# A fused linear attention and MoE kernel: numerators in one PSUM bank and the free columns of the visitor's key-value bank, a visit in five operations, a new order

## The chip, the cores and the metric

The kernel runs on one core of a Trainium2 chip. The metric is the device time in microseconds of one execution. Each statement of a time below is from a run on the chip or from one profiled execution of it.

## What is computed

Per head, keys and queries go through a feature map with an exponential of both signs; keys and values are summed over the sequence into a small matrix kv and a vector z; each query gives a numerator (its features times kv) and a denominator (its features times z). The quotients of 8 batches and 8 heads, 576 tokens of 64 columns each, are the 4608 x 512 input of a feed-forward stage.

```python
def phi(x):
    proj = np.einsum('bhsd,df->bhsf', x, w_phi)
    proj = proj - np.max(np.abs(proj), axis=-1, keepdims=True)
    return np.concatenate([np.exp(proj), np.exp(-proj)], axis=-1)
q_p, k_p = (phi(q), phi(k))
kv = np.einsum('bhsf,bhsd->bhfd', k_p, v)
z = np.sum(k_p, axis=2)
num = np.einsum('bhsf,bhfd->bhsd', q_p, kv)
den = np.einsum('bhsf,bhf->bhs', q_p, z)[..., None] + 1e-06
x = (num / den)          # then 4608 tokens x 512
h = x @ w_in             # 512 -> 1024
e = np.exp(h - h_max); solu = h * e / (e.sum() + 1e-09)
out = layer_norm(solu) * g_ln @ w_out
```

## The kernel before

The attention is cut into 16 units u of four heads, and each unit into two pairs of heads (sub 0 and 1), so there are 32 pairs n = 2u + sub. For a pair, TensorE projects keys and queries (`k_rows`, `q_rows`, `mid_rows`; tiles pjk, pjq, pjm), VectorE takes row maxima off and turns the queries, ScalarE takes exponentials (ek, fq), GpSimd adds up z (zt, zacc), and TensorE makes kv (tile kvT). VectorE turns kv into kvs, SP sends it through DRAM and back as kvf. From the tenth pair on ScalarE and VectorE also make qz, the features weighted with z, for the denominators. TensorE then makes numerators and denominators, ScalarE copies them out (E, dn), VectorE takes reciprocals, SP broadcasts them (rb), and GpSimd divides into xa or xb. The feed-forward works on 36 tiles of 128 tokens: ScalarE and GpSimd split the input in two parts (mxh, mxl), TensorE makes h with 24 matmuls of 512 columns, VectorE and ScalarE make nm, eu and ub, and after a way through DRAM (uTs, uhs, uls) TensorE makes o with 24 more.

PSUM has six banks of 512 fp32 columns under tag a, and one double bank under tag h for h. A kv takes 384 columns of a bank (3F, with F = 128): 256 for kv and 128 for z.

All operations are declared to a `Plan` (L217) in a fixed sequence, each with its engine, what it comes after, and the buffers it takes and uses. `SEQUENCE` (L54) is a list of positions in that declaration: `order` (L235) emits the operations in that order and hands out buffers first in, first out, each when its last user stands earlier in the list. Every engine runs its own operations in that order (`InOrder`, L258), waiting at each for what it needs; a bank that is handed on makes the next user wait until the last reader of the former is done.

The unit of the work around the change is the visit (`visit`, L588), operation V of a pair. For the pairs 0 to 5 it makes kv alone. From pair 6 on (JOIN) a visit is joined: one undivided run on TensorE that holds the numerators of the pair before (`q_num`, L759: two halves of 288 columns, in two banks of tag a), the kv matmuls of its own pair (eight, 256 columns), for sub 0 the four matmuls over the tokens that the two pairs share (vz), the z sums (L617), and the denominators of the pair before (`q_den`, L790, a bank of its own). A joined visit with sub 0 takes five banks at once: two for numerators, two for kv (both pairs of the unit), one for denominators. `q_oe` (L812) copies numerators out in two steps c (qv), `den_eps` the denominators (de), `kv_turn` reads the kv bank (kve).

The visit is declared at L950 to L975, the numerators and denominators and their copies at L1040 to L1056.

Of the kernel before, what the change touches and what calls it, by code (L numbers as in the profile page):

```python
# [54 lines left out]
    2, 119, 1, 120, 77, 79, 93, 121, 122, 82, 83, 309, 86, 310, 131, 137, 134, 103, 104, 123, 124, 84, 94, 95,  # L55
    97, 96, 98, 99, 132, 138, 100, 133, 78, 88, 105, 106, 80, 81, 135, 136, 101, 102, 311, 312, 139, 10, 11, 85,
    125, 91, 185, 4, 5, 92, 176, 109, 126, 127, 128, 129, 130, 111, 112, 89, 90, 313, 107, 108, 211, 212, 215,
    110, 314, 169, 171, 174, 175, 113, 114, 87, 6, 261, 150, 178, 151, 156, 157, 153, 154, 152, 12, 13, 155,
    158, 213, 214, 216, 7, 115, 116, 28, 29, 217, 140, 142, 177, 143, 186, 141, 195, 172, 187, 190, 173, 8, 144,
    117, 145, 193, 194, 9, 118, 196, 189, 192, 223, 188, 226, 180, 183, 181, 30, 191, 218, 43, 44, 3, 221, 229,  # L60
    159, 160, 197, 198, 277, 182, 161, 184, 163, 162, 199, 200, 45, 14, 219, 220, 222, 268, 278, 279, 282, 284,
    22, 23, 280, 283, 46, 281, 224, 227, 31, 170, 201, 24, 25, 225, 228, 269, 231, 164, 179, 230, 203, 204, 202,
    146, 33, 263, 321, 242, 15, 245, 244, 247, 262, 248, 205, 206, 371, 243, 246, 249, 34, 289, 290, 207, 208,
    264, 270, 424, 272, 35, 209, 16, 250, 265, 26, 273, 274, 232, 165, 147, 148, 17, 32, 36, 210, 27, 275, 291,
    276, 315, 166, 18, 380, 233, 236, 237, 149, 167, 168, 38, 285, 286, 238, 425, 525, 251, 271, 322, 253, 266,
    267, 252, 426, 316, 427, 428, 287, 288, 255, 256, 19, 319, 37, 39, 40, 41, 429, 451, 292, 293, 294, 257, 20,
    21, 295, 302, 296, 317, 318, 418, 239, 240, 258, 259, 320, 344, 452, 364, 419, 420, 234, 235, 241, 297, 254,
    260, 48, 303, 47, 42, 49, 50, 323, 381, 382, 383, 421, 1849, 384, 1850, 51, 52, 59, 65, 385, 386, 392, 387,
    393, 366, 324, 325, 326, 422, 423, 327, 304, 345, 367, 328, 330, 331, 333, 369, 430, 370, 390, 368, 388,
    1891, 526, 529, 332, 1851, 329, 389, 74, 527, 528, 530, 68, 391, 298, 1852, 299, 300, 301, 56, 487, 373,  # L70
    375, 478, 488, 1853, 1854, 66, 1892, 378, 374, 489, 471, 491, 490, 431, 334, 335, 1855, 336, 372, 53, 54,
    57, 346, 347, 348, 349, 398, 399, 1858, 400, 305, 338, 1893, 432, 353, 1870, 350, 60, 351, 492, 494, 306,
    354, 307, 308, 339, 1894, 376, 377, 379, 365, 589, 71, 493, 1895, 598, 433, 434, 642, 1859, 62, 355, 537,
    453, 58, 352, 636, 499, 500, 394, 395, 401, 472, 1896, 1897, 1900, 1871, 404, 435, 340, 356, 69, 357, 454,
    538, 405, 406, 1898, 1901, 1872, 1873, 396, 341, 342, 75, 397, 402, 403, 440, 76, 358, 359, 437, 1856, 61,
    72, 438, 55, 1912, 1913, 337, 343, 455, 441, 407, 408, 409, 442, 582, 1874, 473, 474, 1902, 599, 475, 1875,
    1876, 1857, 600, 601, 713, 456, 603, 604, 410, 495, 1903, 436, 637, 496, 505, 1914, 638, 639, 602, 605, 67,
    63, 64, 476, 73, 1904, 1905, 1860, 1861, 439, 70, 480, 411, 1906, 1862, 1863, 477, 479, 539, 640, 540, 641,
    648, 443, 643, 445, 460, 360, 412, 413, 446, 497, 1879, 461, 498, 482, 485, 1907, 1915, 531, 541, 1908,
    1909, 591, 483, 644, 457, 484, 506, 414, 415, 416, 361, 481, 507, 646, 458, 645, 1916, 459, 501, 502, 508,  # L80
    590, 486, 444, 1899, 447, 417, 751, 647, 1864, 1917, 1918, 1919, 1921, 673, 362, 363, 704, 462, 511, 512,
    463, 464, 465, 466, 1865, 1910, 532, 533, 649, 542, 448, 449, 584, 587, 503, 1880, 504, 509, 585, 513, 547,
    586, 606, 510, 820, 1922, 467, 514, 515, 516, 544, 546, 545, 517, 548, 549, 610, 1923, 1866, 450, 611, 468,
    588, 608, 534, 609, 607, 543, 535, 469, 470, 1867, 707, 1933, 1868, 518, 550, 536, 558, 559, 519, 551, 552,
    553, 592, 1924, 1925, 1926, 593, 596, 594, 520, 560, 561, 562, 752, 597, 714, 718, 1954, 1927, 1934, 753,
    754, 715, 717, 716, 755, 616, 617, 1928, 595, 756, 563, 567, 568, 618, 521, 720, 569, 564, 565, 719, 522,
    523, 1935, 1936, 524, 566, 570, 572, 571, 706, 1996, 1929, 573, 1997, 1937, 1938, 674, 583, 1920, 622, 574,
    575, 554, 650, 651, 614, 615, 1877, 612, 1939, 1940, 1941, 652, 653, 658, 660, 697, 828, 613, 619, 708, 555,
    556, 623, 1881, 1998, 1999, 655, 656, 872, 1942, 576, 620, 757, 624, 866, 709, 763, 764, 654, 710, 725,
    1911, 727, 705, 577, 578, 711, 1943, 728, 867, 734, 712, 2000, 1955, 868, 726, 625, 1882, 626, 2017, 699,  # L90
    869, 657, 627, 1930, 2001, 2002, 1883, 1931, 628, 661, 700, 663, 698, 702, 870, 1884, 1885, 557, 2005, 662,
    703, 1956, 1957, 701, 621, 819, 659, 664, 721, 987, 722, 871, 579, 1958, 1959, 1960, 629, 630, 665, 580,
    1886, 667, 666, 729, 730, 812, 814, 1963, 815, 829, 833, 835, 758, 830, 759, 761, 2018, 2006, 675, 676, 677,
    731, 816, 678, 682, 679, 723, 681, 2019, 1932, 680, 683, 684, 765, 631, 760, 668, 724, 732, 733, 981, 581,
    831, 834, 840, 841, 832, 762, 1944, 766, 817, 632, 818, 633, 634, 1878, 635, 685, 767, 687, 669, 735, 1887,
    1888, 821, 1889, 1945, 1946, 686, 1964, 688, 737, 689, 873, 690, 1947, 768, 769, 1948, 1949, 691, 788, 789,
    770, 1961, 1962, 836, 837, 878, 670, 671, 773, 775, 774, 738, 692, 943, 739, 874, 879, 875, 876, 877, 1965,
    982, 985, 983, 984, 986, 2020, 2021, 672, 740, 741, 771, 742, 743, 772, 776, 777, 778, 779, 1950, 1951,
    1952, 693, 903, 694, 695, 1890, 2022, 790, 2023, 2026, 736, 744, 745, 934, 944, 945, 935, 948, 950, 904,
    780, 846, 781, 947, 993, 823, 824, 696, 2059, 2060, 2061, 1966, 1967, 1968, 838, 791, 792, 782, 1869, 839,  # L100
    1953, 1969, 1970, 2101, 2102, 880, 793, 797, 746, 825, 927, 798, 842, 2003, 2004, 2024, 881, 946, 949, 794,
    2027, 2062, 2063, 822, 1971, 1972, 747, 847, 748, 749, 750, 813, 2064, 2080, 2081, 783, 784, 1042, 795,
    2065, 2066, 928, 826, 827, 799, 2068, 796, 800, 801, 844, 843, 2103, 802, 803, 2104, 2105, 2106, 2107, 848,
    852, 853, 905, 936, 2069, 882, 883, 885, 994, 2028, 2110, 2025, 2007, 906, 907, 908, 886, 804, 805, 912,
    854, 1049, 806, 807, 884, 955, 2038, 1975, 1976, 2082, 2083, 1973, 2070, 2084, 988, 938, 2039, 989, 990,
    2085, 2086, 2029, 2030, 2031, 888, 929, 930, 931, 932, 845, 2040, 2041, 2071, 849, 850, 855, 939, 933, 856,
    857, 858, 887, 891, 893, 851, 1096, 2111, 1050, 890, 1102, 956, 2032, 808, 940, 2072, 892, 889, 894, 785,
    786, 953, 954, 991, 992, 2073, 787, 859, 2074, 2033, 1018, 2075, 2008, 995, 996, 895, 896, 897, 1058, 909,
    1097, 911, 1059, 2108, 2009, 860, 861, 951, 952, 2042, 1043, 2067, 961, 1019, 962, 910, 1100, 997, 998, 914,
    862, 863, 864, 963, 941, 865, 1020, 1021, 1060, 1061, 2010, 913, 999, 1063, 1064, 1070, 2089, 2090, 1098,  # L110
    1099, 1101, 1003, 957, 958, 809, 810, 2034, 898, 899, 811, 942, 1005, 1065, 1062, 1108, 1211, 2035, 2036,
    1109, 915, 917, 1022, 1023, 937, 916, 2076, 2077, 0, 2078, 918, 967, 2043, 2044, 2045, 2046, 919, 920, 1044,
    968, 921, 1024, 1025, 1103, 2112, 2113, 2114, 2047, 2011, 1004, 1000, 1002, 1001, 1027, 1977, 1978, 922,
    969, 2115, 2116, 2012, 2079, 959, 2091, 1217, 2087, 2037, 1045, 1046, 923, 960, 964, 1047, 1104, 1105, 970,
    971, 2013, 972, 2014, 973, 1006, 1106, 900, 1029, 1107, 1048, 1979, 1071, 1008, 1009, 901, 1007, 965, 966,
    974, 2092, 1980, 924, 925, 926, 1133, 1028, 1981, 1984, 2015, 1173, 975, 1010, 902, 2122, 1212, 2093, 1213,
    1051, 1053, 1110, 1111, 1054, 1011, 1056, 1164, 2185, 1066, 1067, 1012, 1068, 1069, 1174, 1178, 1175, 1214,
# [1195 lines left out]
```

## Time and profile before

| | us |
|---|---|
| runs, median of 3 | 679.15 |
| lowest and highest | 677.68, 679.55 |
| span of the profiled execution | 675.5 |
| TensorE busy | 664.0 |
| VectorE busy | 504.5 |
| ScalarE busy | 372.5 |
| GpSimd busy | 391.5 |
| first h matmul starts | 72.38 |

The profile lists every instruction with its engine, its operation and its tiles (out <- in). Engines are PE (TensorE), PEld (its weight loads), DVE (VectorE), ACT (ScalarE), POOL (GpSimd) and SP (the queue that issues transfers). Matmuls overlap, and their ends are modelled, so the time from the start of one group to the start of the next tells more than a duration. An fp32 matmul leaves two records, which is why eight kv matmuls are counted as 16. The granted clock of TensorE was full but for a part of the first 20 us.

### The profile page before, as it was taken

The numbers are of one execution on the slowest core, as the hardware profiler recorded it, in microseconds if no ns is written. First come the engines' busy times: TensorE is split into PE (matmuls) and PEld (weight loads), VectorE is DVE, ScalarE is ACT, GpSimd is POOL, SyncE is SP. The second block draws the span as 40 slices with busy tenths as digits, with TensorE's granted clock in tenths as the row PEclk, the third lists the DMA queues.
The fourth block names the chain that finished last, engine by engine and source line by source line (L and its number), as shares of the span: only waits on it lengthen the run. The fifth ranks groups of instructions, "written<-read, shape, count | busy, mean of one in ns | idle before, by whom it ended". The sixth has DMA issues, their size and how long they took to land.

```text
span 675.5 us, 13664 instructions
## 1 busy us (share of the span) xinstructions
PE 664.0 (98%) x4932; PEld 498.1 (74%) x4932; DVE 504.5 (75%) x754; ACT 372.5 (55%) x717; POOL 391.5 (58%) x438
## 2 busy tenths in 40 slices
PE   8999999999999999999999999999999999999998
PEld 6765676777677777777767777877778777788887
DVE  6999989869888777888898886979858644542550
ACT  4897675465655565655656555464654654332231
POOL 0124999677375467575858457746785374464321
PEclk8999999999999999999999999999999999999999
DMA  8767998688687887787879766686875574543202
GB/s 285 259 243 229 268 270 200 216 233 238 204 235 226 243 205 220 196 254 234 234 196 264 225 178 191 200 240 195 220 183 156 169 210 128 157 129 109 79 16 78
DMA packets 135554, 135.34 MB, mean 200 GB/s; under 512 B 59840, under 2 KB 109376, under 8 KB 134976
## 3 DMA queue, kind: packets, MB, share of 16 engines
q1 hardware_dynamic: 135488, 134.48, 68.2%
q8 instruction: 39, 0.64, 0.4%
q14 instruction: 27, 0.22, 0.1%
HBM read 85.53 MB, written 48.91 MB: 199 GB/s over the span
## 4 chain that ended last, share of the span: by engine, by line
PE 82%; DVE 13%; issue 1%; DMA 1%; SPq 1%; ACT 1%; DVEq 0%; ACTq 0%
PE h L266 27%; PE o L266 27%; PE kvT L266 9%; PE num L266 8%; PE pjq L266 3%; DVE m L266 3%; PE pjk L266 3%; DVE dq L266 2%; DVE w L266 2%; PE den L266 2%; DVE dk L266 1%; DVE qz L266 1%; SPq L266 1%; PE pjm L266 1%; DVE dE L266 1%
## 5 line engine op out<-in xcount | busy, mean ns | idle before, releaser
L266 POOL TENSOR_TENSOR uls<-uTs,uhs 128x1024 fp32r<-128x1024 f32 x33 | 79.2, 2401 | 46.0 <-ACT uhs L266 37.2
L266 PE MATMUL o<-w_out_h,uhs 128*128 128x512 f32 x264 | 103.8, 393 | 0.0
L266 PE MATMUL o<-w_out_l,uhs 128*128 128x512 f32 x264 | 102.8, 389 | 0.0
L266 PE MATMUL o<-w_out_h,uls 128*128 128x512 f32 x264 | 102.7, 389 | 0.0
L266 ACT ACTIVATE ek<-dk 128x512 f32<-128x512 f32 (+1 forms) x160 | 86.3, 582 | 23.5 <-DVE dk L266 23.2
L266 PE MATMUL h<-win_h,mxh 128*128 128x512 f32 x288 | 91.9, 400 | 0.0
L266 PE MATMUL h<-win_l,mxh 128*128 128x512 f32 x288 | 89.0, 390 | 0.0
L266 PE MATMUL h<-win_h,mxl 128*128 128x512 f32 x288 | 88.8, 390 | 0.0
L266 ACT ACTIVATE fq<-pT 128x512 f32<-128x512 f32 (+1 forms) x140 | 72.9, 559 | 24.5 <-DMA pT<-dqd 11.2
L266 ACT ACTIVATE eu<-h,nm 128x1024 f32<-128x1024 f32 x36 | 40.1, 1115 | 81.1 <-DVE nm L266 63.5
L266 POOL TENSOR_TENSOR zt<-ek 128x512 f32<-128x512 f32 x52 | 67.1, 1291 | 30.1 <-ACT ek L266 29.4
L266 DVE TENSOR_REDUCE nm<-h 128x1 f32<-128x1024 f32 x36 | 43.9, 1219 | 53.3 <-PE h L266 53.1
L266 PE MATMUL num<-fq,kvf 128*64 128x288 f32 x512 | 69.2, 412 | 1.2 <-DVE dk L266 1.0
L266 PEld LDWEIGHTS h<-win_h,mxh 128*128 128x128 f32 x288 | 51.9, 188 | 14.7 <-issue 0.9
L266 PEld LDWEIGHTS h<-win_l,mxh 128*128 128x128 f32 x288 | 54.1, 188 | 11.6
L266 PEld LDWEIGHTS h<-win_h,mxl 128*128 128x128 f32 x288 | 54.1, 188 | 11.5
L266 PE MATMUL kvT<-ek,rawv 128*64 128x256 f32 x512 | 61.2, 380 | 0.0
L266 DVE TENSOR_TENSOR eu<-h,eu 128x1024 f32<-128x1024 f32 x36 | 43.8, 1217 | 21.6 <-ACT eu L266 19.9
L266 PEld LDWEIGHTS o<-w_out_h,uhs 128*128 128x128 f32 x264 | 49.5, 188 | 11.5 <-issue 0.4
L266 PEld LDWEIGHTS o<-w_out_h,uls 128*128 128x128 f32 x264 | 49.5, 188 | 10.4
L266 PEld LDWEIGHTS o<-w_out_l,uhs 128*128 128x128 f32 x264 | 49.6, 188 | 9.9
L266 PEld LDWEIGHTS num<-fq,kvf 128*64 128x64 f32 x512 | 34.1, 136 | 30.2 <-issue 6.9
(106 smaller groups left out, 1265.4 us busy)
## 6 DMA issues: line engine op xcount, KB each, us to landing
du<-ub SPq DMA_DIRECT2D x33, 512.0 KB, 3.4
uTs<-du SPq DMA_DIRECT2D x132, 128.0 KB, 3.3
rb<-d SPq DMA_DIRECT2D x64, 144.0 KB, 3.7
dqd<-dq SPq DMA_DIRECT2D x14, 640.0 KB, 4.5
pT<-dqd SPq DMA_DIRECT2D x56, 160.0 KB, 4.1
out<-os SPq DMA_DIRECT2D x35, 256.0 KB, 3.1
rawq<-in_q SPq DMA_DIRECT2D x32, 256.0 KB, 4.2
rawk<-in_k SPq DMA_DIRECT2D x32, 256.0 KB, 4.4
```

The lines of the kernel that those rows point to most:

```text
L266: return self.tc.keep_in_program_order(method(*args, **kwargs))
```

## The change

The second half of the numerators no longer has a bank of its own where the pair is visited: the first 448 columns of the numerators go to one bank of tag a, and the last 128 to the columns 384 to 511 of the bank in which the visiting pair makes its kv. For a visitor with sub 0 the numerators open that bank, for sub 1 it was opened by the matmuls over the shared tokens. ScalarE copies 448 and 128 columns in place of twice 288.

The visit is taken apart into five operations of the plan, which other work can stand between: the numerators (qo), the kv matmuls (K), the matmuls over the shared tokens (rest, once per unit), the z sums (Z), and the denominators (qd). Each has its own conditions. K comes after the numerators that share its bank; rest after K of sub 0; K of sub 1 after rest; Z after K and rest; qd after the features and kv, or from the tenth pair on after qz alone. The bank of the second kv of a unit is taken at rest and not at the start of the visit. The number of planned operations goes from 2601 to 2701, and `SEQUENCE` is a new list for all engines; the instructions on the engines are of the same kinds and numbers, apart from the widths named.

In the new list the copy of the last 128 numerators stands ahead of the visitor's K at pairs 6 and 25 and between K and rest at pairs 9, 21 and 23 (the pair whose numerators they are, plus one, is the visitor; the pair is named by its numerators), and behind Z at the other 21.

```diff
-    def visit(st, sub, before):
-        if before:
-            q_num(*before)
-        if sub == 0:
-            for i in range(2):
-                st["kv", i] = bank(KV_TAG, [P, 512], "kvT")
+    def kv_open(st, sub):
+        st["kv", sub] = bank(KV_TAG, [P, 512], "kvT")
+
+    def kv_mm(st, sub, opens):
+        if opens:
+            kv_open(st, sub)
         for t in range(4):
...
-        for i in range(0 if sub else 2):
+    def kv_rest(st):
+        kv_open(st, 1)
+        for i in range(2):
             for j, r in enumerate(HEADS):
...
-        tiles = list(key_tiles(st, sub))
+    def z_sums(st, sub):
         if st["u"] in Z_PE:
-            z_mm(st, sub, tiles)
+            z_mm(st, sub, list(key_tiles(st, sub)))
         else:
             kv_z(st, sub)
-        if before:
-            q_den(*before)
...
-    def q_num(st, sub):
-        for c in range(2):
-            kvf = st["kvf", sub]
-            po = st["num", sub, c] = bank("a", [P, 512], "num")
+    def q_num(st, sub, host):
+        kvf, first = st["kvf", sub], bank("a", [P, 512], "num")
+        if host is None:
+            second, cut, starts = bank("a", [P, 512], "num"), HC, True
+        else:
+            hst, hsub = host
+            if hsub == 0:
+                kv_open(hst, 0)
+            second, cut, starts = hst["kv", hsub][:, 3 * F :], S - F, hsub == 0
+        st["num", sub] = [(first, slice(0, cut)), (second, slice(cut, S))]
+        for c, (po, cs) in enumerate(st["num", sub]):
             for s in range(2):
                 for j, r in enumerate(HEADS):
                     nc.tensor.matmul(
-                        po[r, :HC], lhsT=kvf[:, s, r], rhs=st["qf", sub, s][:, j, c * HC : (c + 1) * HC],
-                        start=(s == 0), stop=(s == 1),
+                        po[r, : cs.stop - cs.start], lhsT=kvf[:, s, r], rhs=st["qf", sub, s][:, j, cs],
+                        start=(s == 0 and (c == 0 or starts)), stop=(s == 1), skip_group_check=True,
                     )
...
+            after = [("ke", 2 * sub, x, 1) for x in range(2)] + [("vl", 2 * sub)]
+            after += [("rest",)] if sub else []
+            after += [("abs", (pu, "qo", ps_))] if hosts else []
+            add(("K", sub), "tensor", 4 * mm32(256), z, kv_mm, (sub, sub == 0 and not hosts), after,
+                [] if sub or hosts else [(KV_TAG, ("kv", 0))], tiles)
+            if sub == 0:
+                add(("rest",), "tensor", mm32(256), z, kv_rest, (), [("K", 0), ("ke", 1, None, 1), ("vl", 1)],
+                    [(KV_TAG, ("kv", 1))], [("e", 1, None), ("rv", 1), ("kv", 0)])
...
+                add(("Z", sub), "tensor", mm32(128), z, z_sums, (sub,), [("K", sub), ("rest",), ("zh", sub)], (),
+                    [("za", sub), ("kv", sub)])
...
+            add(("qd", sub), "tensor", (1 if scaled(n) else 2) * mm32(HC), z + 5.5, q_den, (sub,),
+                [("abs", x) for x in sums(n)] if scaled(n) else feat, [("a", ("den", sub))],
+                [("G", sub)] if scaled(n) else fk)
             for c in range(2):
                 add(("qv", sub, c), "scalar", act(HC, True), z + 5.1 + c, q_oe, (sub, c),
-                    [source["num"]] + ([("qv", sub, 0)] if c else []), () if c else [("E", ("E", sub))],
-                    [("num", sub, c), ("E", sub)])
+                    [("qo", sub)] + ([("qv", sub, 0)] if c else []), () if c else [("E", ("E", sub))],
+                    [ht if c else ("num", sub, 0), ("E", sub)])
```

## Rows read from the trace of the kernel before

**Rows 1.** The page's first part: busy us (share of the span) xinstructions.
```profile
PE 664.0 (98%) x4932; PEld 498.1 (74%) x4932; DVE 504.5 (75%) x754; ACT 372.5 (55%) x717; POOL 391.5 (58%) x438
```

**Rows 2.** Windows: start:end, length, busy PE, PEld, DVE, ACT, POOL, clock, DMA, GB/s.
```profile
10.00:72.00 62.00, 59.55 (x784) 40.56 (x782) 60.49 (x101) 49.59 (x96) 18.59 (x10) 0.97 0.78 258
72.00:250.00 178.00, 174.68 (x1333) 128.74 (x1330) 149.31 (x225) 107.97 (x216) 124.97 (x134) 1.00 0.81 231
```

**Rows 3.** Chain that ended last, in order of time: start us, us, what.
```profile
129.48 0.89 PE pjk L266 x16
...
317.60 5.44 PE h L266 x24
```

**Rows 4.** Waits of PE: engine line waited for: us in total, times, longest.
```profile
PE pjm L266 <- DVE kvs L266: 1.6, 1, 1.6
...
PE pjk L266 <- DVE dq L266: 0.5, 1, 0.5
PE pjk L266 <- DVE kvs L266: 0.5, 1, 0.5
```

**Rows 5.** Timeline of PE: start us, us, instruction [idle before it <- releaser].
```profile
32.27 2.16 PE L266 MATMUL num<-fq,kvf 128*64 128x288 f32 x16
34.36 1.18 PE L266 MATMUL den<-fq,kvf 128*32 128x288 f32 x16
...
322.97 2.16 PE L266 MATMUL num<-fq,kvf 128*64 128x288 f32 x16
324.96 1.90 PE L266 MATMUL kvT<-ek,rawv 128*64 128x256 f32 x16
326.79 0.43 PE L266 MATMUL kvT<-zacc,ones 128*32 128x128 f32 x8
```

**Rows 6.** Timelines of POOL and PE, up to the first h.
```profile
62.48 2.38 POOL L266 TENSOR_TENSOR win_l<-w,win_h 128x1024 fp32r<-128x1024 f32 x1 [7.31 <-ACT win_h L266]
65.72 2.92 POOL L266 TENSOR_TENSOR xa<-E,rb 128x576 f32<-128x576 f32 x2 [0.85 <-DMA rb<-d]
69.36 1.27 POOL L266 TENSOR_TENSOR mxl<-xa,mxh 128x512 fp32r<-128x512 f32 x1 [0.73 <-ACT mxh L266]
...
72.38 0.73 PE L266 MATMUL h<-win_h,mxh 128*128 128x512 f32 x2
```

**Rows 7.** Timelines of DVE and PE around 103 us.
```profile
102.58 1.22 DVE L266 TENSOR_TENSOR eu<-h,eu 128x1024 f32<-128x1024 f32 x1
...
102.78 1.13 PE L266 MATMUL pjq<-wph,rawq 64*128 64x128 f32 x14 [0.98 <-DVE dk L266]
103.86 0.73 PE L266 MATMUL h<-win_h,mxh 128*128 128x512 f32 x2
```

**Rows 8.** Timelines of DVE and PE around 178 us.
```profile
174.30 2.57 DVE L266 SCALAR_TENSOR_TENSOR qz<-fq,kvf,qz 128x576 f32<-128x576 f32 x1 [0.17 <-ACT fq L266]
...
181.71 0.49 PE L266 MATMUL pjm<-wph,rawk 64*128 64x128 f32 x4 [1.57 <-DVE kvs L266]
```

**Rows 9.** Timelines of PE, ACT and DVE around 344 us.
```profile
343.14 0.67 PE L266 MATMUL den<-qz,ones 128*32 128x288 f32 x8
343.88 0.41 ACT L266 ACTIVATE dn<-den 128x288 f32<-128x288 f32 x1 [3.73 <-PE den L266]
344.78 0.53 DVE L266 STREAM_TRANSPOSE kvs<-kvT 128x384 f32<-128x384 f32 x1
345.37 1.16 PE L266 MATMUL pjk<-wph,rawk 64*128 64x128 f32 x16 [0.47 <-DVE kvs L266]
```

**Rows 10.** Groups of ACT by form: xcount, busy us, mean ns, idle before.
```profile
L266 ACT COPY E<-num 128x288 f32<-128x288 f32 x64 | 24.2, 397 | 17.2 <-PE num L266 7.5 <-POOL xb L266 5.7 <-POOL xa L266 3.8
L266 ACT ACTIVATE fq<-pm 128x128 f32<-128x128 f32 x28 | 8.1, 298 | 0.0
```

**Rows 11.** Timelines of PE and ACT around 418 us.
```profile
415.64 2.16 PE L266 MATMUL num<-fq,kvf 128*64 128x288 f32 x16
...
421.86 0.39 ACT L266 COPY E<-num 128x288 f32<-128x288 f32 x1
```

More of the change, by code (lines that the diff above doesn't have):

```diff
@@ L814, in q_oe @@
             st["nums", sub] = sb("E", [P, S], name="E")
-        nc.scalar.copy(out=st["nums", sub][:, c * HC : (c + 1) * HC], in_=st["num", sub, c][:, :HC])
+        po, cs = st["num", sub][c]
+        nc.scalar.copy(out=st["nums", sub][:, cs], in_=po[:, : cs.stop - cs.start])
     def den_eps(st, sub):
@@ L860, in linear_attention_then_moe @@
     divides = {}
-    states = {}
+    states = {u: {"u": u, "b": u // 2, "qd": u % 2} for u in range(2 * B)}
     def keys_values(n):
@@ L951, in linear_attention_then_moe @@
             n = 2 * u + sub
-            joined = n >= JOIN
             z = 4.0 + 4.5 * sub
-            cost = (4 if sub else 5) * mm32(256) + SWITCH + (5 * mm32(128) if u in Z_PE else mm32(128))
             pu, ps_ = (n - 1) // 2, (n - 1) % 2
-            feats = [(2 * sub, 0), (2 * sub, 1), (1, None)]
-            after = [("ke", *x, 1) for x in feats] + [("vl", 2 * sub), ("vl", 1)]
-            tiles = [("e", *x) for x in feats] + [("rv", 2 * sub)] + ([("kv", 1)] if sub else [("rv", 1)])
@@ L959, in linear_attention_then_moe @@
-            alloc, early = [] if sub else [(KV_TAG, ("kv", i)) for i in range(2)], {}
-            if sub:
-                after.append(("V", 0))
-            if u not in Z_PE:
-                after.append(("zh", sub))
-                tiles.append(("za", sub))
-            if joined:
-                after += [("abs", x) for x in features(n - 1) + keys_values(n - 1) + sums(n - 1)]
-                tiles += [("abs", (pu, "f", ps_, s)) for s in range(2)] + [("abs", (pu, "kf", ps_))]
-                tiles += [("abs", (pu, "G", ps_))] if scaled(n - 1) else []
-                alloc = [("a", ("abs", (pu, "num", ps_, c))) for c in range(2)] + alloc + [("a", ("abs", (pu, "den", ps_)))]
-                den = (1 if scaled(n - 1) else 2) * mm32(HC)
-                early = {(pu, "qv", ps_, c): den + cost + (1 - c) * 2 * mm32(HC) for c in range(2)}
-                early[u, "kve", sub] = den
-                cost += 4 * mm32(HC) + den
@@ L974, in linear_attention_then_moe @@
-            add(("V", sub), "tensor", cost, z, visit, (sub, (states[pu], ps_) if joined else None), after, alloc, tiles,
-                early)
-            prev = ("V", sub)
+            hosts = JOIN <= n
+            after = [("ke", 2 * sub, x, 1) for x in range(2)] + [("vl", 2 * sub)]
+            tiles = [("e", 2 * sub, x) for x in range(2)] + [("rv", 2 * sub), ("kv", sub)]
+            after += [("rest",)] if sub else []
+            after += [("abs", (pu, "qo", ps_))] if hosts else []
+            add(("K", sub), "tensor", 4 * mm32(256), z, kv_mm, (sub, sub == 0 and not hosts), after,
+                [] if sub or hosts else [(KV_TAG, ("kv", 0))], tiles)
@@ new lines, in linear_attention_then_moe @@
+            if sub == 0:
+                add(("rest",), "tensor", mm32(256), z, kv_rest, (), [("K", 0), ("ke", 1, None, 1), ("vl", 1)],
+                    [(KV_TAG, ("kv", 1))], [("e", 1, None), ("rv", 1), ("kv", 0)])
+            if u in Z_PE:
+                add(("Z", sub), "tensor", 5 * mm32(128), z, z_sums, (sub,), [("K", sub), ("rest",)], (),
+                    [("e", 2 * sub, x) for x in range(2)] + [("e", 1, None), ("kv", sub)])
+            else:
+                add(("Z", sub), "tensor", mm32(128), z, z_sums, (sub,), [("K", sub), ("rest",), ("zh", sub)], (),
+                    [("za", sub), ("kv", sub)])
@@ L1040, in linear_attention_then_moe @@
             feat, fk = [("abs", x) for x in features(n) + keys_values(n)], [("f", sub, 0), ("f", sub, 1), ("kf", sub)]
+            hu, hs = (n + 1) // 2, (n + 1) % 2
             joined = JOIN <= n + 1 < 4 * B
-            visitor = ("abs", ((n + 1) // 2, "V", (n + 1) % 2))
-            source = {"num": visitor if joined else ("qo", sub), "den": visitor if joined else ("qd", sub)}
-            if not joined:
-                add(("qo", sub), "tensor", 4 * mm32(HC), z + 5.0, q_num, (sub,), feat,
-                    [("a", ("num", sub, c)) for c in range(2)], fk,
-                    {(u, "qv", sub, 0): 2 * mm32(HC)})
-                add(("qd", sub), "tensor", (1 if scaled(n) else 2) * mm32(HC), z + 5.5, q_den, (sub,),
-                    feat + [source["num"]] + [("abs", x) for x in sums(n)], [("a", ("den", sub))],
-                    fk + ([("G", sub)] if scaled(n) else []))
+            host, ht = ((states[hu], hs), ("abs", (hu, "kv", hs))) if joined else (None, ("num", sub, 1))
+            add(("qo", sub), "tensor", 4 * mm32(HC), z + 5.0, q_num, (sub, host),
+                feat + ([("abs", (hu, "rest"))] if joined and hs else []),
+                [("a", ("num", sub, 0))] + ([] if joined and hs else [(KV_TAG if joined else "a", ht)]),
+                fk + ([ht] if joined and hs else []))
+            add(("qd", sub), "tensor", (1 if scaled(n) else 2) * mm32(HC), z + 5.5, q_den, (sub,),
+                [("abs", x) for x in sums(n)] if scaled(n) else feat, [("a", ("den", sub))],
+                [("G", sub)] if scaled(n) else fk)
             for c in range(2):
                 add(("qv", sub, c), "scalar", act(HC, True), z + 5.1 + c, q_oe, (sub, c),
-                    [source["num"]] + ([("qv", sub, 0)] if c else []), () if c else [("E", ("E", sub))],
-                    [("num", sub, c), ("E", sub)])
-            add(("de", sub), "scalar", act(HC, True), z + 6.2, den_eps, (sub,), [source["den"]], [("dE", ("dn", sub))],
+                    [("qo", sub)] + ([("qv", sub, 0)] if c else []), () if c else [("E", ("E", sub))],
+                    [ht if c else ("num", sub, 0), ("E", sub)])
+            add(("de", sub), "scalar", act(HC, True), z + 6.2, den_eps, (sub,), [("qd", sub)], [("dE", ("dn", sub))],
                 [("den", sub)])
```

3 lines of the change are left out of this document (2 added, 1 removed), and 276 rows, old and new, of the table SEQUENCE.

## The prediction

> **What bounds the kernel now.** Three views, in this order. The page's busy shares put TensorE at 98% of the span [rows 1]. A busy TensorE need not be at its peak, so the chain of work comes next: from the first h to the last o it is almost wholly TensorE, and a tile's 24 h matmuls of 512 columns take 5.44 us, 227 ns each, where 512 columns at 2.4 GHz are 213 ns [rows 3]. So it is full. The windows by stage show the one other limit: from 10 to 72 us VectorE is busy 60.49 of 62 us and TensorE only 59.55; from 72 to 250 us it is the other way round [rows 2]. What TensorE waits for after the first h is short: 1.0, 1.6, 0.5 and 0.5 us, 3.6 in all, each time for a bank that VectorE had still to empty [rows 4, 7]. More than that, and what the start can give, can't be won without taking work off TensorE.
>
> How I set the two orders side by side: I wrote out TensorE's operations in both, gave each the duration that its kind has in the trace (for instance 5.44 for a tile's h and 0.89 for a projection [rows 3], 1.99 for the numerators and 1.83 for the kv matmuls, from start to start [rows 5]), and read off how much TensorE work lies between two operations. That gives distances, not a time for the whole.
>
> **Part 1, the tiling mode changes of TensorE.** The numerators are followed by kv matmuls of the same 128*64 tile after 1.99 us, and by the 128*32 denominators after 2.09 us [rows 5]: 0.10 us for a change of tile. Counted in the two orders, up to the first h there are 47 changes before and 33 after, and behind it 139 and 140. The operations ahead of the first h are the same in both, and behind it both hold 593.4 us of TensorE work. So this saves 14 x 0.10 = 1.4 us, all in the stretch where VectorE is the full engine [rows 2]. I give it nothing of its own; it is a bound of part 2. Splitting the numerators 448 + 128 in place of 288 + 288 leaves 16 records per visit and the same columns; nothing.
>
> **Part 2, the start of the first h.** It starts at 72.38 and its last input, mxl, had landed at 70.63 [rows 6]. In the new order GpSimd has the last win_l piece behind the two divides instead of ahead of them. Divides end at 68.64; then win_l 2.38 and mxl 1.27 [rows 6], ending at 72.3. But the reciprocal that the divides wait for has 51.7 us of VectorE work ahead of it in the new order and 52.6 in the old (each operation by its kind's mean, scaled to the busy time), and VectorE has hardly a gap there [rows 2], so all this comes 0.9 us earlier: first h at 71.5, **-0.9 us**. Bounds: 0 if the divides don't come earlier (their rows wait for a transfer, so SP's queue, whose order is new too, may hold them), and -1.4 if only TensorE's own work counts. What is late next is the projections' evacuation on VectorE, which is as full as before.
>
> **Part 3, the waits behind the first h.** The 0.98 us at 102.78 is a projection that takes a bank 0.45 us after the one that filled it [rows 7]. In the new order two other operations lie between; this wait goes. What is late next is the h bank, of which there is one: eu ends at 103.80 and h starts at 103.86 [rows 7]. Its chain is 3.8 us from the end of the last h; the new order leaves 3.75 us of work in place of 2.56. So 0.9 of it goes. The 0.5 us wait for dq stays, as the same three projections stand in the same order. The two waits for kvs, 1.57 and 0.47, are banks of a kv asked for again soon. Such places with under 1.5 us of TensorE work between number nine before, of which these two waited, and seven after: 7 x 2.04 / 9 = 1.6, so 0.45 goes. Which one waits is a matter of what VectorE has in front of its kvs: at 181 us a qz that took 2.57 us [rows 8], where most take about 0.8. Together **-1.3 us**; bounds -2.9 (none waits) and +1.8 (three of seven at 1.57). The hand-overs as a whole don't become roomier: 28 banks are asked for again within 2 us after the first 60 us, 26 before. The new order spends the bank that it gains. That only the denominators wait for qz now gains nothing either, since none of these waits names qz [rows 4, 7]. Transfers: SP's queue carries each kv back to its numerators, and the least TensorE work between a kv's Z and its numerators is 8.6 us in both orders, so nothing there.
>
> **Part 4, what the shared bank adds.** In 26 visits ScalarE now copies the last 128 numerators out of a bank that TensorE is still to write (K, rest, Z) and that VectorE is to read (kve). In the trace of before every reader starts behind the last write into its bank, as dn 0.07 us behind den [rows 9], and no bank has two engines at work in it at once, so no row gives the price. Where the copy stands behind Z in the order, in 21 of the visits, it costs TensorE nothing whatever the rule. In five it stands ahead of K (numerators 6 and 25) or between K and rest (9, 21, 23), and if the bank as a whole is handed over, as it is in every row of before, TensorE waits. At 9 a projection of 0.89 lies between and covers it; at the other four nothing does. Price of one: TensorE's end to ScalarE's start 0.07 [rows 9], the copy, and for the way back VectorE's end to TensorE's start, 0.06 [rows 9]. A copy of 288 columns is 0.40, an exp of 128 columns 0.30 [rows 10]; I take the 0.30, nearest in size. 0.43 each, four times: **+1.7 us**. Bounds: 0 (no ordering), and 7.3 if ScalarE is late with its copy as it often is: the second copy starts at once in 10 of 23 visits from 120 to 550 us, over 2.5 us late in 7, 1.4 on average; the rows show the latest, 4.2 us behind the numerators' end [rows 11]. 4 x (0.43 + 1.4) = 7.3. I take the low price since in two of the four ScalarE has the kv matmuls' 1.83 us to catch up. In 11 visits VectorE's kve stands behind that copy in the order; VectorE has room after 72 us [rows 2], so nothing, at worst +2 with what queues behind it on VectorE (maxima and differences, for which the next K waits).
>
> Nothing in these rows shows that a read and a write of different columns of one bank must be kept apart. The Trainium skill ("PSUM — Partial Sum Buffer", section "PSUM bank collisions raise a hardware error") says that two engines in one bank and 32-partition quadrant collide even at disjoint columns, so that software must order them; no row here shows it. By that rule part 4 is the 1.7 us, without it 0.
>
> **Sum** against the profiled span of 675.5 us, which is 3.65 below the median of the three runs, 679.15: -0.9 - 1.3 + 1.7 = -0.5, so 678.7 us by the runs' measure. Tail: the last tiles' order changes, but the nearest hand-over there (a tile's transposes to its o) goes from 5.4 to 8.2 us of work, so nothing.
>
> **Rivals.** (a) *No measurable change*, as summed: 678.7. (b) *The waits go and the shared bank is free*: -1.4 - 2.9 + 0 = -4.3, 674.9 us. For it: the kvs waits hang on one slow VectorE instruction each and the new order needs no repeat of that; against it: seven equally short hand-overs. (c) *ScalarE's late copies hold TensorE*: the 7.3 of part 4, -0.9 - 1.3 + 7.3 = +5.1, 684.3 us. For it: 7 late copies in 23 [rows 11] are in-order ScalarE waiting for other engines, and TensorE's queue now stands behind such a copy; against it: only four places. It is slower from 0.63 us of lateness per place: 4 x (0.43 + 0.63) - 2.2 = +2.04. (d) *The change doesn't loosen anything*: the same short hand-overs; that is inside (a).
>
> **How the numbers follow.** A measurement of this kernel tells 0.3% (2.0 us) from no change. (a) 0.39, (b) 0.36, (c) 0.25; these are also the chances of same, faster and slower, since (b) and (c) stand for all between them and 2.0 us. The range takes (a) with its bounds and most of (b) and (c): 673.0 to 685.0; (a) alone is 677.1 to 681.2.
>
> **What would show it.** After: the first h near 71.5 in the timeline; no TensorE wait of 1 us near 102; TensorE waits named "ACT E" of about 0.4 us, four of them, at numerators 6, 21, 23 and 25 (none: the bank is not ordered; 1 us or more: (c)); as many waits for kvs as before, one or two. The prediction is wrong in kind if waits for VectorE behind the first h pass 6 us, or if the first h starts after 73.

## The result, and the profile after

The changed kernel takes 688.85 us (686.32 to 689.5, 4 runs), the kernel before 678.41 on the same chip: ratio 1.015, 95% interval 1.0128 to 1.0172. It is slower by 10.4 us, and outside my range of 673.0 to 685.0. The profiled execution took 688.89 us, with a span of 687.0 against 675.5.

The page's first part and the windows by stage, after (columns as in [rows 1, 2]):

```profile
PE 666.9 (97%) x4932; PEld 496.1 (72%) x4932; DVE 500.3 (73%) x754; ACT 371.3 (54%) x717; POOL 391.0 (57%) x438
...
72.00:250.00 178.00, 174.66 (x1328) 126.35 (x1328) 147.10 (x228) 106.28 (x216) 129.51 (x140) 1.00 0.80 229
250.00:600.00 350.00, 340.45 (x2346) 251.67 (x2343) 255.58 (x374) 187.14 (x363) 211.56 (x230) 1.00 0.68 196
```

The same stretch of the kernel before:

```profile
250.00:600.00 350.00, 349.53 (x2404) 261.66 (x2403) 263.10 (x385) 191.32 (x368) 223.76 (x246) 1.00 0.71 201
```

From the first h to the end, before and then after:

```profile
72.38:675.50 603.12, 595.98 (x4081) 450.98 (x4080) 439.01 (x645) 320.00 (x617) 371.22 (x415) 1.00 0.68 194
```
```profile
69.54:687.00 617.46, 601.27 (x4082) 450.14 (x4080) 437.04 (x647) 320.25 (x620) 373.33 (x417) 1.00 0.65 189
```

From 72 to 250 us TensorE is busy as long as before (174.66 us against 174.68 [rows 2]). From 250 to 600 it stands still for 9.6 us where it stood for 0.5. The first h starts 2.84 us earlier (69.54 against 72.38 [rows 6]). Up to the first h of tile 15 TensorE has the same operations to do in both orders, and there 0.42 us of this lead is left (329.69 against 330.11 us). The other 11.9 us are lost behind it.

The 11.5 us of span are the sum of three parts: the earlier first h, -2.8; TensorE's waits behind it, 12.8 us in the table where there were 3.8, +9.0; and TensorE's busy time for the same matmuls, 601.27 in place of 595.98, +5.3. Of the last, 1.7 us is a lower clock (below); the other 3.6 us stays open.

The waits of TensorE after (total, times, longest), to set beside [rows 4]:

```profile
PE den L272 <- DVE qz L272: 3.8, 2, 3.0
PE num L272 <- DMA kvf<-dk: 2.5, 2, 1.4
PE kvT L272 <- ACT E L272: 2.2, 4, 1.1
```

None of the three was there behind the first h before. The waits for VectorE to empty a bank, which I had counted on to shrink, did: 0.7 for dq and 0.6 for kvs are left of 3.6.

**The worst place.** Timelines of VectorE, GpSimd and TensorE around 343 us, after:

```profile
337.35 1.29 POOL L272 TENSOR_TENSOR zacc<-zacc,ek 64x512 f32<-64x512 f32 x1
338.50 4.45 DVE L272 SCALAR_TENSOR_TENSOR qz<-fq,kvf,qz 128x576 f32<-128x576 f32 x1
338.60 1.41 POOL L272 TENSOR_TENSOR xa<-E,rb 128x576 f32<-128x576 f32 x1
339.96 2.36 POOL L272 TENSOR_TENSOR uls<-uTs,uhs 128x1024 fp32r<-128x1024 f32 x1
342.41 0.58 POOL L272 TENSOR_SCALAR sa<-sm 128x1 f32<-128x1 f32 x1
342.86 1.50 DVE L272 STREAM_TRANSPOSE dq<-dq 128x1280 f32<-128x1280 f32 x1
344.29 1.72 DVE L272 SCALAR_TENSOR_TENSOR qz<-fq,kvf,qz 128x576 f32<-128x576 f32 x1
345.94 0.57 DVE L272 STREAM_TRANSPOSE kvs<-kvT 128x384 f32<-128x384 f32 x1
...
346.07 0.69 PE L272 MATMUL den<-qz,ones 128*32 128x288 f32 x8 [2.97 <-DVE qz L272]
```

A qz takes 0.8 us in most rows. This one is done just behind the end of GpSimd's xa and uls: it begins while a zacc runs, and both of the next large GpSimd instructions come before it. The second qz (1.72) ends after a zt. The denominators of pair 19 stand in TensorE's queue and wait 2.97 us.

So long a qz isn't new. In the kernel before the first qz of this same pair took 4.45 us too. First the shortest, median and longest qz there in ns, then the timelines, with both qz of the pair in one row:

```profile
L266 DVE SCALAR_TENSOR_TENSOR qz<-fq,kvf,qz x46: 778/817/4445, 149.6 to 582.2; 128x576 f32<-128x576 f32 x46
```
```profile
336.65 5.65 DVE L266 SCALAR_TENSOR_TENSOR qz<-fq,kvf,qz 128x576 f32<-128x576 f32 x2
336.86 2.39 POOL L266 TENSOR_TENSOR uls<-uTs,uhs 128x1024 fp32r<-128x1024 f32 x1
338.49 2.16 PE L266 MATMUL num<-fq,kvf 128*64 128x288 f32 x16
339.21 1.27 POOL L266 TENSOR_TENSOR zt<-ek 128x512 f32<-128x512 f32 x1
```

There both were done at 342.30, and the denominators started at 343.14 [rows 9] without a wait. TensorE is at the same point in both kernels (the numerators start at 338.49 before and at 338.26 after). What is new is where qz stands on VectorE: the first starts 1.85 us later, and a dq transpose of 1.50 us comes between the two.

Behind the wait TensorE has half its clock (windows: start:end, length, busy PE, PEld, DVE, ACT, POOL, clock, DMA, GB/s):

```profile
343.00:347.00 4.00, 1.03 (x16) 0.47 (x14) 3.51 (x3) 0.38 (x2) 3.60 (x7) 1.00 0.63 198
347.00:351.00 4.00, 4.00 (x35) 3.63 (x32) 3.01 (x6) 3.34 (x8) 0.54 (x4) 0.57 0.61 165
```

A granted clock of 0.57 over 4 us is 43% of 4 us lost, 1.7 us more. Behind 72 us the clock was 1.00 in the profiled execution of the kernel before. The wait and the clock at this one place come to 4.7 of the 11.5 us of span.

**The shared bank.** TensorE waits for ACT E at 106.15, 387.89, 427.55 and 476.81 us (0.42, 0.36, 0.35, 1.08), at the numerators 6, 21, 23 and 25, as forecast. What I hadn't seen is ScalarE and VectorE. Timelines at 364 us, after:

```profile
364.17 0.57 DVE L272 STREAM_TRANSPOSE kvs<-kvT 128x384 f32<-128x384 f32 x1
364.78 0.27 ACT L272 COPY E<-kvT 128x128 f32<-128x128 f32 x1 [3.81 <-DVE kvs L272]
365.10 1.16 PE L272 MATMUL pjk<-wph,rawk 64*128 64x128 f32 x14 [0.30 <-ACT E L272]
365.99 0.40 ACT L272 ACTIVATE dn<-den 128x288 f32<-128x288 f32 x1
366.45 0.38 PE L272 MATMUL pjm<-wph,rawk 64*128 64x128 f32 x2 [0.19 <-ACT dn L272]
```

ScalarE's copy and VectorE's kvs read different columns of one bank, and one starts when the other has ended. In all 26 visits no copy overlaps the kvs of its bank; in ten the gap is under 0.07 us. This is the order that the program keeps, and it agrees with the Trainium skill ("PSUM — Partial Sum Buffer", section "PSUM bank collisions raise a hardware error"), by which two engines that both read count too. No run here shows what the chip would do without it. I cited that section for TensorE's writes alone.

### The profile page after: what moved, and what is told of

It reads as the page before. It is cut to its first block, busy times and chain, and to the rows that moved or that the text cites. A ratio compares the mean times of both kernels' runs of the same rounds, so it can differ in the third digit from the quotient of the medians.

```text
span 687.0 us, 13659 instructions
## 1 busy us (share of the span) xinstructions
PE 666.9 (97%) x4932; PEld 496.1 (72%) x4932; DVE 500.3 (73%) x754; ACT 371.3 (54%) x717; POOL 391.0 (57%) x438
## 4 chain that ended last, share of the span: by engine, by line
PE 62%; DVE 17%; DMA 8%; SPq 6%; ACT 3%; issue 3%; POOL 1%; DVEq 0%; ACTq 0%; POOLq 0%
PE h L272 23%; PE o L272 19%; PE kvT L272 8%; SPq L272 6%; PE num L272 5%; DVE m L272 4%; DVE dq L272 3%; DVE qz L272 2%; DMA kvf<-dk 2%; PE pjk L272 2%; PE pjq L272 2%; DVE w L272 2%; DVE dk L272 2%; PE den L272 2%; DVE nm L272 1%
## 5 line engine op out<-in xcount | busy, mean ns | idle before, releaser
L272 ACT ACTIVATE ek<-dk 128x512 f32<-128x512 f32 (+1 forms) x160 | 89.4, 585 | 30.6 <-DVE dk L272 26.7
L272 POOL TENSOR_TENSOR xa<-E,rb 128x576 f32<-128x576 f32 (+1 forms) x32 | 29.0, 908 | 111.8 <-DMA rb<-d 70.8
L272 ACT ACTIVATE fq<-pT 128x512 f32<-128x512 f32 (+1 forms) x140 | 74.7, 561 | 14.7 <-DMA pT<-dqd 5.8
L272 PE MATMUL num<-fq,kvf 128*64 128x448 f32 (+1 forms) x304 | 57.6, 507 | 3.3 <-DMA kvf<-dk 2.5
L272 DVE SCALAR_TENSOR_TENSOR qz<-fq,kvf,qz 128x576 f32<-128x576 f32 x46 | 49.5, 1097 | 13.5 <-ACT qz L272 10.5
```

What stands on the lines that cost most here:

```text
L272: return self.tc.keep_in_program_order(method(*args, **kwargs))
```

## The experiments

A list is edited by operation names: qo numerators, K, rest, Z the parts of a visit, qd denominators, de their copy, dc the reciprocal, qv the copies of numerators, kve the kvs, sg and vg the qz of ScalarE and VectorE, ul uls, xl mxl, dv a divide, sc the scale of a tile, kvi the transfers of kvf, kp and qp projections, tb and var a tile's transpose and statistics. The others (ql, ds, bo, qbi) are transfers on SP. The kernel before ran beside every group of runs, on the same chip: 678.3 to 679.1 us.

**Order or mechanism.** Each old visit becomes qo, K, rest, Z, qd side by side, the rest of the old list stays (e1). Then with banks of their own for the second half of the numerators, as before (e6), or with the second copy on VectorE right behind kvs (e7, and e8 in the new order):

```diff
 e6:  hosts = JOIN <= n and n - 1 not in OWN      # OWN: all pairs
 e7:  -nc.scalar.copy(out=st["nums", sub][:, cs], ...)
      +copy = nc.scalar.copy if c == 0 or cs.start == HC else nc.vector.tensor_copy
      list: ... kve, (u, qv, sub, 1), ...
```

> The five operations and the shared bank of the changed kernel, in the order of the kernel before (each old visit written as qo, K, rest, Z, qd side by side). Theory A, the new order is what costs: about 678 to 681 us, since the copy of the last 128 numerators never stands ahead of K here, the denominators keep their lead behind qz, and only ScalarE and VectorE can hold each other up at the shared bank. Theory B, the shared bank or the split itself costs: 685 us or more, with TensorE waits for ACT E or kvs in many visits.

> The old order with the five operations (e1_oldorder), but the numerators in two banks of their own, 288 and 288 columns, as in the kernel before. Theory S, what e1_oldorder loses against the kernel before (3.9 us) comes from sharing the bank: the time of the kernel before, 678 to 679.5 us, and no wait of ScalarE or VectorE for each other at a kv. Rival, writing the visit as five operations costs by itself: 681.5 us or more.

> The old order with the shared bank (e1_oldorder), but the copy of the last 128 numerators on VectorE, right behind its kvs from the same bank, so that one engine reads the bank and neither waits for the other. Theory S, the loss at the shared bank is two engines that read it one after the other (ScalarE idle 12.9 us for kvs, VectorE idle 13.0 us for the copy): 678.5 to 680.5 us, although VectorE gets 26 copies of some 0.2 us more. Rival, what costs is that the bank comes free later or that VectorE's extra work delays the projections' banks: 682 us or more.

> The same copy on VectorE behind kvs, in the new order. It also takes the copy away from ahead of K at pairs 6, 21, 23 and 25. Theory S for the changed kernel as well: about 4 us less than 689, 685 us, the rest being the order. Rival, in the new order VectorE is what binds from 280 to 390 us, so more work on it costs as much as is won: 688 us or more.

| | us | ratio to before |
|---|---|---|
| e1, old order, shared bank | 682.62 | 1.0053 (1.0035 to 1.0072) |
| e6, old order, own banks | 678.39 | 1.0011 (0.9991 to 1.003) |
| e7, old order, shared, copy on VectorE | 679.14 | 1.0015 (0.9998 to 1.0032) |
| e8, new order, shared, copy on VectorE | 689.55 | 1.0168 (1.012 to 1.0217) |

Writing the visit as five operations costs nothing (e6). Sharing the bank costs 3 to 4 us in the old order (4.2 by the medians of e1 and e6, about 3 by their ratios). With one engine to read the bank the loss is gone (e7), which speaks for the two readers; e7 also takes 26 copies off ScalarE, and no run separates the two. The waits of ScalarE and VectorE for each other in e1, all absent before:

```profile
ACT E L272 <- DVE kvs L272: 12.9, 8, 2.6
DVE kvs L272 <- ACT E L272: 13.0, 9, 3.3
```

VectorE doesn't stand longer in all ahead of kvs: it waited 30.1 us there for TensorE before, and in e1 17.5 for TensorE and 13.0 for ScalarE. The price reaches TensorE where the bank is wanted next, as here in e1 (0.83 us):

```profile
183.30 0.27 ACT L272 COPY E<-kvT 128x128 f32<-128x128 f32 x1 [1.05 <-DVE kvs L272]
...
183.62 1.16 PE L272 MATMUL pjq<-wph,rawq 64*128 64x128 f32 x14 [0.83 <-ACT E L272]
```

The order costs 6 us with the copy on ScalarE (688.85 less 682.62), 10 with it on VectorE (689.55 less 679.14). e8 missed: in the new order the same cure gave nothing.

**Where the order loses.** e12 follows the new list up to the z sums of pair 19 (some 326 us; the expectation names pair 20) and the old one for all that is left, with the copies as in e7.

```diff
 e12: new[:1490] + [x for x in old if x not in new[:1490]]
```

> The new order up to TensorE's z sums of pair 20 (some 325 us in the changed kernel's trace), and the old order for all that is left; the copy of the last 128 numerators on VectorE as in e7_oldvec (679.1) and e8_newvec (689.6). Theory, all that the new order loses against the old one is lost behind 330 us (in the two traces TensorE stands at the same work within 1 us at 335 us): 677.5 to 680 us. Rival, the loss is made ahead of it and only shows there (transfers and queues that run late): 684 us or more.

679.33 us, 1.0017 (0.9999 to 1.0036). Against e8, which has the same copies, the loss is made behind 326 us, not carried there.

**One wait at a time.** e2 moves qd, de and dc of pair 19 behind h of tile 15; e3 moves the copies of pairs 6, 21, 23 and 25 behind Z (the line below is for 6 and 25; at 21 and 23 the copy stood between K and rest); e4 does both, and qd of pair 21.

```diff
 e2: -Z(10,0) qd(9,1) de(9,1) kp(11,2) qp(11,2) h(15)
     +Z(10,0) kp(11,2) qp(11,2) h(15) qd(9,1) de(9,1)
 e3: -qo qv,0 qv,1 K Z          +qo qv,0 K Z qv,1
```

> The changed kernel with one visit altered: the denominators of pair 19 (and their copy and reciprocal) stand two projections and half an h later. Theory A, the 2.97 us wait for qz at 346 us and the half clock of 3.2 us behind it (some 1.7 us) are a loss of their own: 4.7 us less than the changed kernel, about 684 us, and a granted clock of 1.00 from 340 to 356 us. Rival, the chain has left TensorE there and the next input is late as well: at most 2 us less, 687 us, with a new wait within 20 us behind.

> The changed kernel with the copy of the last 128 numerators of pairs 6, 21, 23 and 25 behind the visitor's z sums on ScalarE, as at the other visits. Theory A, the four TensorE waits named ACT E (0.42, 0.36, 0.35 and 1.08 us) are the price of the order at the shared bank: 2.2 us less, 686.6 us, and none of the four left. Rival, ScalarE's lateness only moves on to kvs and the projections behind: less than 1 us, 688 us.

> Both of the foregoing, and the denominators of pair 21 (0.80 us wait for qz) two projections later. Theory A, the waits add up: 4.7 + 2.2 + 1.0 = 7.9 us less than the changed kernel, 681 us. Rival, other late inputs take their place: 685 us or more.

689.86, 690.46 and 689.16 us: nothing. My theory, that each wait is a loss of its own, fails in all three. In e2 the denominators no longer wait, but a projection does, since kvs stands behind the two qz on VectorE; TensorE, e2:

```profile
346.37 1.16 PE L272 MATMUL pjq<-wph,rawq 64*128 64x128 f32 x14 [2.14 <-DVE kvs L272]
```

and the clock was 0.50 from 348 to 350 us again. The cause sat one engine further back.

**The held-up qz.** e5 sets GpSimd's small sc operations of tile 16 between xa and uls, e13 ahead of both. Nothing else is changed.

```diff
 GpSimd, after: dv(8,1) ul(9) sc(16)
 e5:            dv(8,1) sc(16) ul(9)
 e13:           sc(16) dv(8,1) ul(9)
```

> The changed kernel with one swap on GpSimd alone: the four small operations that make sc (tile 16) stand ahead of a uls (tile 9) and not behind it, so that GpSimd has no two large two-operand instructions in a row while VectorE makes the first qz of pair 19. Theory H, a qz can't run while GpSimd works on such an instruction, and the 4.45 us qz at 338.5 us is one that found no gap: the qz takes about 2.1 us, VectorE is 2.4 us earlier, the wait for qz at 346 us falls from 2.97 to about 0.6 us, the granted clock stays at 1.00, and the time is 3 to 4.5 us less than the changed kernel's 689, about 685 us. Rival, VectorE's length there has another cause, or the next late input takes the place of this one as it did when only the denominators were moved: 688 us or more.

> The changed kernel with the four small GpSimd operations of sc (tile 16) ahead of the division of pair 17 (xa, 338.6 us), so that GpSimd has small work when VectorE's first qz of pair 19 is due. Theory H: this qz takes about 1 us, not 4.45; TensorE's wait for qz at 346 us and the half clock behind it go; 4 to 5 us less than the changed kernel's 689, about 684.5 us (e5_pool, which left GpSimd one such instruction beside each qz, gave 3). Rival, tightness: another wait follows and no more than e5_pool's gain is left, 686 us or more.

e5: 685.88 us, 1.012 (1.0083 to 1.0157), an interval that still touches the changed kernel's; e13: 684.84, 1.0088 (1.0063 to 1.0113), which is clear of it. The first qz of pair 19, in e5 and then in e13:

```profile
340.64 2.18 DVE L272 SCALAR_TENSOR_TENSOR qz<-fq,kvf,qz 128x576 f32<-128x576 f32 x1
```
```profile
341.82 0.82 DVE L272 SCALAR_TENSOR_TENSOR qz<-fq,kvf,qz 128x576 f32<-128x576 f32 x1 [0.22 <-ACT qz L272]
```

In e5 one instruction (xa) is left beside it and it takes 2.18, in e13 none and it takes 0.82; there TensorE is busy without a gap from 341 to 353 us at a clock of 1.00. Four small GpSimd operations, moved by one place or two, are worth 3 to 4 us of the 10.

**The lead of qz.** From the timelines of the four engines I took, for pairs 9 to 30, the mean time from the end of kvs to the start of the denominators, and cut it up (an issue counts by its end):

| us | kvs to dk issued | to last kvf issued | to ScalarE's first qz | to its last | to VectorE's last | to denominators | sum |
|---|---|---|---|---|---|---|---|
| before | 0.4 | 6.6 | 2.8 | 1.7 | 2.2 | 4.8 | 18.5 |
| after | 0.4 | 8.0 | 2.8 | 2.8 | 3.4 | 1.7 | 19.0 |

The new order keeps the whole and spends the slack at its end: SP, ScalarE and VectorE each do other things in between. To test it, e10 puts VectorE's two qz of every pair directly ahead of the denominators in the old order with own banks; e9 puts the qz of both engines ahead of the numerators in the new order; e11 is e9 with the copies of e8.

```diff
 e10: -vg vg ... qo K rest Z qd             +qo K rest Z vg vg qd
 e9:  -sg sg qo ... vg vg qd   (most pairs)  +sg sg vg vg qo ... qd
```

> The opposite: the old order with own banks (e6_own, 678.4 us) with the two VectorE operations of qz of every pair directly ahead of the pair's denominators, behind the visitor's z sums. Theory L: the lead falls to about 1 us or nothing, TensorE waits for qz in several visits, and the time is 3 to 7 us more, 681.5 to 685.5 us. Rival, the lead doesn't matter: under 680 us.

> The changed kernel (shared bank and copies as they are) with the qz operations of ScalarE and VectorE of every pair ahead of the pair's numerators in the list, as the order before had them. Theory L, the new order loses because qz is made after the numerators and not ahead of them, so that the lead of qz before the denominators falls from about 4.8 to 1.2 us (medians of the profiled executions) and a qz that GpSimd holds up reaches TensorE: no wait of TensorE for qz, no clock under 1.00, and 5 to 6 us less than the changed kernel's 689, about 683.5 us. Rival, VectorE is full from 280 to 390 us and something else on it comes late in its place: 687 us or more.

> The changed kernel with both: qz ahead of the numerators (e9_early), and the copy of the last 128 numerators on VectorE behind kvs (e8_newvec). If both losses are what the theories say, and add up: 689 less 5.5 less 3.4, about 680 us. Rival, more work on VectorE in the new order costs what it gives (e8_newvec gave nothing): the time of e9_early or more.

e10: 689.62 us, 1.016 (1.0136 to 1.0184), 11.2 us more than e6, with TensorE's wait

```profile
PE den L273 <- DVE qz L273: 6.7, 6, 1.8
```

and a granted clock of 0.58 from 217 to 221 us. So the lead is needed. Its mean doesn't rank the kernels, though: reckoned in the same way it is 2.6 us in e10, more than the 1.7 of the changed kernel, and e10 is as slow; it ran out in six places. And e9 fell the other way: 700.04 us, and e11 697.93. ScalarE and VectorE work in order, and in e9 they wait longer for kvf and for each other with their other work queued behind (after: 26.4 and 10.5 us for the same two; before: 30.7 and 11.3); waits in e9:

```profile
ACT qz L272 <- DMA kvf<-dk: 37.9, 14, 8.2
DVE qz L272 <- ACT qz L272: 28.6, 15, 4.1
```

A place further up the list isn't a lead if the data isn't there. That this makes the 11 us is argued and not shown: the kernel before waited 30.7 us for kvf and lost nothing by it.

**A sum of places, or tight everywhere.** e14 is e13 with the copy on VectorE and four more waits taken at their place; e15 is e14 with the copies on ScalarE, behind Z; e16 is e14 with the two qz of pair 29 side by side ahead of other VectorE work.

```diff
 e14, SP:      kvi(4,0) ahead of ql(7,0) ds(3,1) ql(6,1);  kvi(14,1) ahead of bo(28) qbi(15,0,1)
 e14, GpSimd:  ul(28) ahead of dv(14,1);  ul(15) behind xl(17)
 e16, VectorE: -tb(29) vg(14,1,0) var(28) vg(14,1,1)   +vg(14,1,0) vg(14,1,1) tb(29) var(28)
```

> e13_gap, the copy of the last 128 numerators on VectorE (e7_oldvec), and the four longest of the other waits behind 120 us taken at their place: two kvf transfers ahead of others on SP (pairs 8 and 29), one uls ahead of a division on GpSimd (tile 28), one uls behind an mxl (tile 15, beside the qz of pair 21). Theory, a sum of places: 4.7 + 3.1 (waits for ACT E and the late bank at 365 us) + 2.5 + 1.3 + 1.0 = 12.6 us less than 689, 676.5 us, under the kernel before. Rival, tightness: new waits for VectorE and transfers take their place, 682 us or more.

> e14_all with the copies on ScalarE as in the changed kernel, those of pairs 6, 21, 23 and 25 behind the z sums as in e3_copies. Theory S, ScalarE and VectorE read the shared bank one after the other here too: 3 to 4 us more than e14_all. Rival, it matters in the old order alone: within 1.5 us of e14_all.

> e14_all with the two qz of pair 29 on VectorE side by side, ahead of a ub transpose and of the statistics of tile 28, where GpSimd has no large instruction. Theory, a sum of places: no wait for qz at 548 us and no half clock behind it, 4 us less than e14_all's 681.2, 677 us, no slower than the kernel before. Rival, tightness: a new wait takes its place, 680 us or more.

| | us | ratio to before |
|---|---|---|
| e14 | 681.15 | 1.0035 (1.0003 to 1.0067) |
| e15 | 682.56 | 1.0054 (1.003 to 1.0077) |
| e16 | 680.06 | 1.0012 (0.9997 to 1.0027) |

Between my two theories: of 12.6 us expected in e14, 7.7 came. In e14 the same event sat at a new place, two qz held by a uls and an mxl, and a granted clock of 0.58 from 550 to 554 us:

```profile
545.10 2.85 DVE L272 SCALAR_TENSOR_TENSOR qz<-fq,kvf,qz 128x576 f32<-128x576 f32 x1
...
551.09 0.70 PE L272 MATMUL den<-qz,ones 128*32 128x288 f32 x3 [2.41 <-DVE qz L272]
```

In e16 it is gone (two qz of 0.82 each), and the new order is within 0.3% of the kernel before. No version is faster than the kernel before. With the same copies on VectorE, e8 and e16 differ only in some ten operations of GpSimd, SP and VectorE, moved by a few places each: 9.5 us. The copy on VectorE itself is worth 1.4 us there at most (e15 less e14; the two intervals overlap).

## Why the prediction was wrong, point by point

- **Parts 1 and 2, the start: the sign was right, the size and the chain weren't.** The first h starts at 69.54, not 71.5; before it was 72.38 [rows 6]. The two divides ran 2.0 us earlier (63.73 against 65.72 [rows 6]); I had given them 0.9. But the first h doesn't wait for mxl, the end of my chain. Before, it started 1.75 us after mxl was done [rows 6]; after, it starts 0.5 us ahead of that, and in both TensorE goes from its own work into h without a gap:

```profile
68.78 1.28 POOL L272 TENSOR_TENSOR mxl<-xa,mxh 128x512 fp32r<-128x512 f32 x1
68.98 1.13 PE L272 MATMUL cmall<-cmp,spread 128*128 128x512 f32 x2
69.54 1.03 PE L272 MATMUL h<-win_h,mxh 128*128 128x512 f32 x2
```

  So my reason for the sign didn't hold, and that it came right was in part luck. The 1.4 us of fewer tile changes, which I had as a bound only, would be half of the 2.84; no run took it alone.
- **Part 1, "behind it both hold 593.4 us of TensorE work": failed.** The matmuls are the same, but TensorE was busy with them for 601.27 us and not 595.98. Half clock is 1.7 of the 5.3. What the other 3.6 is stays open: e16 has it against e6 as well (600.01 and 596.46 us from the first h on, no lower clock in either there). Changes of tile aren't more: the traces have 135 before and 132 after behind the first h, where I had counted 139 and 140.
- **Part 3, the banks: right.** The 0.98 at 102 us is gone, dq's wait stayed (0.7), one kvs wait of 0.6 at 255 us is left where I expected one or two. -1.3 was forecast; 3.6 less 1.3 is -2.3.
- **Part 3, "only the denominators wait for qz now gains nothing": the step that failed.** I looked at what the freedom could give and not at what the new list does with it. The lead was 4.8 us before and absorbed slow qz: the 2.57 us of [rows 8], a row that I used for something else, and the 4.45 us of pair 19, where 0.84 us of lead was left. With 1.7 us of lead a qz that GpSimd holds up reaches TensorE. Price: 3.8 us of waits and 1.7 of half clock; e13, which mends one place alone, gives 4 back.
- **Part 3, the transfers on SP, "so nothing there": failed.** The least TensorE work from Z to numerators is the same in both, and yet kvf was late twice (1.37 at 134.65, 1.12 at 551.75). What differs is what SP issues in between: on average 1.4 us more from dk to the last kvf.
- **Part 4, the four places: right in kind and size** (2.2 us against 1.7; 0.42, 0.36 and 0.35 for three of them, 1.08 for the fourth). But they can't be had back by moving the copies (e3), as the engines behind them were late anyway.
- **Part 4, the other visits: failed.** I weighed the copy against TensorE's writes and gave 0 to the visits in which kvs stands behind the copy. In the other 15 the copy stands behind kvs, and I didn't look at them. With two readers in turn the bank comes free later, and either engine waits for the other with its queue behind it: 3 to 4 us in the old order (e1 less e6), where I had "at worst +2". In the new order its share is 1.4 at most (e15 less e14) or nothing (e8 against the changed kernel); that other inputs are late there as well would explain it, but isn't shown.
- **The rivals.** (c) gave 684.3 for late ScalarE copies in front of TensorE; they cost 2.2, not 7.3. No rival had a lead that is used up, none had the clock, and the bounds on the slow side were all of banks. So the range was too narrow there, for want of a mechanism, not of a size. The sign that I set for being wrong in kind, over 6 us of waits for VectorE behind the first h, didn't show it either: they came to 5.7, with the time 10 us off.

What stays open: the 3.6 us of longer TensorE work; and e14 gave 5 us less than the list of its waits promised. One part was the wait of 2.41 us and the lower clock at 551 us, for which e16 gained 1.1; what makes up the rest isn't settled. Whether some order with the shared bank beats the kernel before isn't settled either; the best here equals it.

## What to carry to other kernels

When a change lets an instruction wait for less, work out for each queue how far ahead of its consumer the input will now be made, and set the slowest instance of that input against this lead, not the usual one. Count two readers of one buffer as a hand-over too, if the program or the chip lets one engine at a time at it: in the old order a copy by the engine that reads there anyway was free, by another engine it cost 3 to 4 us. Mending single waits tells little when an engine further back is the late one; the row to look for is the longest instance of an instruction that is usually short.

## What the runs showed of the hardware

- VectorE's qz and GpSimd's large two-operand instructions ran one after the other. All eleven groups of qz rows after that average over 1.0 us a piece have such an instruction beside them; the longest let two pass (4.45 us, the end of a zacc, xa and uls, then the qz itself). The Trainium skill ("SBUF — State Buffer", section "Who interferes with whom") says that a VectorE instruction with two SBUF inputs and a GpSimd instruction that reads SBUF exclude each other for a whole instruction. The traces agree, with 4.45, 2.18 and 0.82 us for two, one and none beside it (after, e5, e13). They also show a waiting qz passed over by the next GpSimd instruction, before as well (4.45 us, past a uls and a zt).
- TensorE's granted clock fell to 0.50 (1.2 GHz) in the middle of a full kernel, for some 3 to 4 us each time: behind a wait of 2.97 us (after), 2.14 (e2), 1.69 (e5) and 2.41 (e14); in e9 for 7 us at a stretch, twice. A wait of 1.58 us had it behind it in e12, one of 2.13 in e4 did not, so the length of the wait alone doesn't decide. In the profiled execution of the kernel before, whose longest wait behind the first h was 1.57 us, it never fell there, nor in that of e16. Where it fell, it cost some 1.7 us on top of the wait, which the table of waits doesn't show.
